# Transposes of an attention unit in one step, output transposes of global pairs joined with the next pair's, later loads of the globals, and a new order, in a fused attention and MLP kernel

## The chip, the cores and the metric

The kernel runs on one core of a Trainium2 chip. A core has five engines that run side by side, each through its own list of instructions in order: TensorE (PE in the profile) multiplies and transposes, VectorE (DVE), ScalarE (ACT) and GpSimd (POOL) work on elements, SyncE (SP) issues most of the DMAs here. The metric is the device time of one execution in microseconds (us). Before the change it is 1034.27 us, the median of three runs (1033.44 to 1035.80).

## What is computed

Attention over 8 batches, 8 heads, 512 local and 32 global positions, head size 64. A local query sees the 32 global keys and the local keys within 32 positions; a global query sees all 544 keys. Each batch's outputs, heads side by side, are 544 tokens of 512 numbers, 4352 tokens in all. They go through an MLP with a hidden size of 2048.

```python
s_g = scale * np.matmul(q_g, k_all.transpose(0, 1, 3, 2))
out_g = np.matmul(sm(s_g), v_all)
s_ll = np.where(mask, scale * np.matmul(q_l, k_l.transpose(0, 1, 3, 2)), -1000000000.0)
s_l = np.concatenate([scale * np.matmul(q_l, k_g.transpose(0, 1, 3, 2)), s_ll], axis=-1)
out_l = np.matmul(sm(s_l), np.concatenate([v_g, v_l], axis=2))
x = attn_out.transpose(0, 2, 1, 3).reshape(B * S, H * D)
h = x @ w_in
g = 0.5 * h * (1.0 + erf(h * inv_sqrt2))
return g @ w_out
```

## The kernel before

**Work.** The attention is cut into 64 *units* `(b, half, p)`: batch, half of the 512 local queries (256), pair of heads. The MLP runs in 17 *passes* over 256 tokens each: sixteen keyed `(b, half)`, and a last one, `"g"`, with the global tokens of all batches. Where numbers must stay exact to float32, a value is split into a high and a low part in a faster format (`fp32r`) and three products are summed; the first 12 units work in plain float32 instead.

**Steps.** All work is written as named steps, each with its function, engine, due time, what it needs, which buffers it takes and frees. The names that matter here:

- `lk`, `lq`, `lv`: loads of a unit's keys, queries and values (`lv` of unit (0,0,0) and of (0,1,0) load those of four units, into `vre`); `lg`: a batch's global queries and keys; `glv`: values for a global pair. All but one are issued by SP.
- `tk`, `tq`: transposes of keys and queries; `k1`, `q1`: copies of them; `s`: scores; `m`: mask and row minimum (DVE); `e`: exponential (ACT); `n`, `nf`, `ns`: normalisation (DVE, POOL).
- `t`: transposes of the normalised attention, `st_t` (L712). Seven matmuls of 128x128: four with j = 0, three with j = 1, each half into one slot of the PSUM pool `t`, which has two. `ah`, `al`: copies of them as high and low part (`ao` tiles in the first 12 units, `at` later); `o`: attention times values, whose results take slots of the same pool; `c`, `x`: sums of the results (tile `xs`).
- For a global pair `g = (b, x)` of four heads, with i = 0, 1 for its two head pairs: `gt`: five transposes of its attention (`gu_t`); `go`: times values; `gsh`, `gsl`: the result's parts summed into `os`; `gx`: its transpose (`gu_x`), one matmul; `gyh`, `gyl`, `gw`: parts summed (tile `gc`) and written to a DRAM buffer, from which the last pass starts.
- `wl`: load of one of 32 weight tiles of 0.5 MB (`wpair`, even numbers w_in, odd ones w_out); `w1`, `w2` (ACT), `w3` (DVE), `w4` (DVE or ACT), `w5` (DVE or POOL): the split of a pair of them. Pair n is made of weights n and n + 1 (n even) and belongs to hidden block f = n / 2. Five raw buffers serve the sixteen pairs.
- `h` (or `hc`, in quarters): up-projection of one hidden block, twelve matmuls (L963 to L965), tile `h`; `g`, `gh`, `gl`: its Gelu and the two parts; `mo`: down-projection, six matmuls (L995 to L997), tile `acc`.

**Order.** A planner walks through the steps when the program is built. It keeps a clock for each engine from the table of durations `DUR` and a model of the DMA from the loads' `size`, and of the steps that can start first it takes the one that is due first. Due times come from formulas, plus offsets by kind of step (`OFF`, `OFF0`) and by single step (`XO`). The result is one fixed order, and each engine runs its list strictly in it. So a step that waits holds up everything behind it on its engine.

**Start.** For the first 110 us the first eight units, the weights and the first pass run together. All of `w_in` and `w_out` stays on the chip afterwards.

Of the kernel before, what the change touches and what calls it, by code (L numbers as in the profile page):

```python
# [109 lines left out]
    ('gn', (0, 0)): -484.33, ('gn', (0, 1)): 234.3, ('go', (0, 0), 0): -396.25, ('go', (0, 0), 1): -58.92,  # L110
    ('go', (0, 1), 0): 174.43, ('go', (0, 1), 1): 24.38, ('gsh', (0, 0), 0): 229.87, ('gsh', (0, 0), 1): -56.02,
    ('gsh', (0, 1), 0): 290.46, ('gsh', (0, 1), 1): -341.29, ('gsl', (0, 0), 0): -143.39, ('gsl', (0, 0), 1): -123.39,
    ('gsl', (0, 1), 0): -70.91, ('gsl', (0, 1), 1): -75.86, ('gt', (0, 0)): -197.62, ('gt', (0, 1)): -44.95,
    ('gvc', (0, 0), 0): 575.55, ('gvc', (0, 0), 1): 539.98, ('gvc', (0, 1), 0): -62.66, ('gvc', (0, 1), 1): 295.35,
# [1339 lines left out]
```

## Time and profile before

| | |
|---|---|
| median of three runs | 1034.27 us |
| profiled execution | 1035.02 us |
| its span, first to last instruction | 1033.2 us |
| moved by DMA | 71.17 MB |
| mean granted clock of PE | 0.99 |

The page's slices (40 of 25.8 us each; a digit is the busy share in tenths) show a start that differs from the rest:

```profile
PE   7789999999999999999999999999999999999998
ACT  6789738888899989798899989888999979873231
PEclk9789999999999999999999999999999999999999
GB/s 195 245 165 292 55 38 64 65 61 75 48 36 66 58 73 39 68 56 71 46 37 65 60 71 39 70 55 72 43 40 59 65 71 47 33 24 43 1 22 21
```

In the first four slices the weights are loaded, PE is not yet full, and its granted clock is below full speed at times. From the fifth on PE is full and the DMA moves little. How long a group of instructions takes is read from the table by lines (count, busy time, mean duration of one, and the idle time ahead of it with what ended it), and what happened at a place from the timeline (start, duration, engine, line, operation, what it writes and reads).

### The profile page before, as it was taken

Reading aid. Unit: us, or ns where it says so; the run is one execution under the profiler, and the core shown is the slowest. Engines: PE = TensorE matmul, PEld = TensorE weight load, DVE = VectorE, ACT = ScalarE, POOL = GpSimd, SP = SyncE. Lnnn points to the kernel's source line nnn. Section 1 sums busy time; section 2 is a strip of 40 time slices with the busy share of each in tenths; the row PEclk is TensorE's granted clock in tenths of the full one; section 3 lists DMA queues with packets and bytes.
Section 4 is the critical chain, followed back from the end, with each engine's and each line's share of the span. In section 5 each row is a group of like instructions: output and inputs, shape, how many; then the busy total and the mean of one; then the engine's idle time right before and its main releaser. Section 6 shows DMA issues by size and latency. Waiting matters only on the chain.

```text
span 1033.2 us, 21240 instructions
## 1 busy us (share of the span) xinstructions
PE 1011.6 (98%) x6908; PEld 909.9 (88%) x6908; DVE 734.2 (71%) x2169; ACT 814.9 (79%) x1761; POOL 352.8 (34%) x399
## 2 busy tenths in 40 slices
PE   7789999999999999999999999999999999999998
PEld 4478888999999999999999999999999999999897
DVE  5688628896888988766888988866888888751000
ACT  6789738888899989798899989888999979873231
POOL 3332433343323433343323443343323443332221
PEclk9789999999999999999999999999999999999999
DMA  8869213333223232323222332323222332111000
GB/s 195 245 165 292 55 38 64 65 61 75 48 36 66 58 73 39 68 56 71 46 37 65 60 71 39 70 55 72 43 40 59 65 71 47 33 24 43 1 22 21
DMA packets 273135, 71.17 MB, mean 69 GB/s; under 512 B 258304, under 2 KB 266496, under 8 KB 273024
## 3 DMA queue, kind: packets, MB, share of 16 engines
q1 hardware_dynamic: 271872, 69.42, 29.3%
q8 instruction: 55, 0.90, 0.4%
q14 instruction: 56, 0.46, 0.2%
q10 hardware_dynamic: 1152, 0.39, 0.1%
HBM read 60.29 MB, written 9.44 MB: 67 GB/s over the span
## 4 chain that ended last, share of the span: by engine, by line
PE 93%; SPq 2%; DMA 2%; DVE 1%; ACT 1%; issue 0%; POOL 0%; ACTq 0%; DVEq 0%
PE h L963 12%; PE h L965 12%; PE h L964 12%; PE acc L995 12%; PE acc L996 12%; PE acc L997 12%; PE s L646 5%; PE o L753 5%; PE t L717 3%; PE go L886 2%; DMA wpair<-in_moe_w_out_dram 2%; PE sg L797 1%; PE t L718 1%; PE o L766 1%; PE gt L847 1%; PE t L720 1%
## 5 line engine op out<-in xcount | busy, mean ns | idle before, releaser
L311 POOL TENSOR_TENSOR gl<-gf,gh 128x512 fp32r<-128x512 f32 x135 | 179.3, 1328 | 421.7 <-ACT gh L301 306.0
L963 PE MATMUL h<-xx,w 128*128 128x256 f32 x1088 | 311.9, 287 | 1.8 <-DVE w L303 1.8
L965 PE MATMUL h<-xx,w 128*128 128x256 f32 x1088 | 304.2, 280 | 0.8 <-DVE w L311 0.8
L964 PE MATMUL h<-xx,w 128*128 128x256 f32 x1088 | 303.7, 279 | 0.0
L995 PE MATMUL acc<-w,gh 128*128 128x512 f32 x544 | 219.6, 404 | 0.0
L963 PEld LDWEIGHTS h<-xx,w 128*128 128x128 f32 x1088 | 204.8, 188 | 12.7 <-issue 3.3
L997 PE MATMUL acc<-w,gh 128*128 128x512 f32 x544 | 214.7, 395 | 0.0
L996 PE MATMUL acc<-w,gl 128*128 128x512 f32 x544 | 214.6, 395 | 0.0
L964 PEld LDWEIGHTS h<-xx,w 128*128 128x128 f32 x1088 | 205.0, 188 | 6.8
L965 PEld LDWEIGHTS h<-xx,w 128*128 128x128 f32 x1088 | 204.5, 188 | 1.0 <-DVE w L311 1.0
L481 ACT ACT_TABLE_LOAD x139 | 178.3, 1283 | 6.5 <-PE h L965 4.2
L481 ACT ACTIVATE gf<-h 128x512 f32<-128x512 f32 x136 | 81.4, 598 | 68.5 <-PE h L965 56.6
L997 PEld LDWEIGHTS acc<-w,gh 128*128 128x128 f32 x544 | 102.1, 188 | 24.5
L996 PEld LDWEIGHTS acc<-w,gl 128*128 128x128 f32 x544 | 102.5, 189 | 12.8 <-POOL gl L311 0.3
L995 PEld LDWEIGHTS acc<-w,gh 128*128 128x128 f32 x544 | 102.2, 188 | 12.9 <-issue 0.3
L481 ACT ACTIVATE a_t<-a_t,sm 128x192 f32<-128x192 f32 x240 | 109.9, 460 | 1.1 <-DVE sm L665 0.2
L311 POOL TENSOR_TENSOR vs<-vr,vs 128x512 fp32r<-128x512 f32 x52 | 68.5, 1317 | 105.1 <-DVE vs L303 47.1
L301 ACT ACTIVATE gh<-gf 128x512 fp32r<-128x512 f32 x110 | 69.4, 631 | 24.3 <-PE acc L997 21.6
L665 DVE CUSTOM_DVE_ANT_0 a_t<-s,mask 128x192 f32<-128x192 f32 x240 | 76.2, 368 | 16.7 <-PE s L646 15.9
L737 DVE TENSOR_TENSOR at<-t,at 128x512 fp32r<-128x512 f32 (+1 forms) x104 | 62.5, 615 | 28.3 <-ACT at L301 27.9
L301 ACT ACTIVATE at<-t 128x512 fp32r<-128x512 f32 (+1 forms) x104 | 54.1, 540 | 32.2 <-PE t L718 15.7
L311 POOL TENSOR_TENSOR vgs<-raws,vgs 128x640 fp32r<-128x640 f32 x32 | 51.1, 1597 | 77.3 <-ACT vgs L301 68.5
(148 smaller groups left out, 1730.2 us busy)
## 6 DMA issues: line engine op xcount, KB each, us to landing
wpair<-in_moe_w_in_dram SPq DMA_DIRECT2D x16, 512.0 KB, 5.9
wpair<-in_moe_w_out_dram SPq DMA_DIRECT2D x16, 512.0 KB, 6.3
...
raws<-in_k_l_dram SPq DMA_DIRECT2D x224, 36.0 KB, 2.0
raws<-in_q_l_dram SPq DMA_DIRECT2D x224, 32.0 KB, 1.9
...
```

The lines of the kernel that those rows point to most:

```text
L301: nc.scalar.activation(out=out, in_=in_, func=AF.Copy)
L311: (nc.vector if e == "v" else nc.gpsimd).tensor_sub(**kw)
L481: nc.scalar.activation(func=func, **kw)
L646: nc.tensor.matmul(out=st[u, "s", jj][:, c:c + w], lhsT=l, rhs=r, start=(i == 0 and n == 0), stop=(i == 1 and (plain or n == 1)), skip_gro ...
L665: nc.vector.tensor_tensor_reduce(out=a_t[:, j, aoff[half][i]:aoff[half][i] + w], in0=s[:, c:c + w], in1=masks[half][:, c:c + w], scale=-SC ...
L737: nc.vector.tensor_sub(out=at[:, 1], in0=st.pop((u, "t", j))[:, :n * P].rearrange("p (n q) -> p n q", q=P), in1=at.bitcast(F32)[:, 0])
L963: nc.tensor.matmul(out=h, lhsT=hi, rhs=xh, start=(c == 0), stop=False, skip_group_check=True)
L964: nc.tensor.matmul(out=h, lhsT=hi, rhs=xl, start=False, stop=False, skip_group_check=True)
L965: nc.tensor.matmul(out=h, lhsT=lo, rhs=xh, start=False, stop=(c == NCC - 1), skip_group_check=True)
L995: nc.tensor.matmul(out=acc[t], lhsT=gh[:, f % 2, tsl], rhs=hi, start=(f == a), stop=False)
L996: nc.tensor.matmul(out=acc[t], lhsT=gl[:, f % 2, tsl], rhs=hi, start=False, stop=False)
L997: nc.tensor.matmul(out=acc[t], lhsT=gh[:, f % 2, tsl], rhs=lo, start=False, stop=(f == b - 1))
```

## The change

Three edits of the code, new numbers for the planner, and the order that follows from them.

1. From the 13th unit on, the two `t` steps become one, `st_tt`, which issues the same seven transposes and takes both slots of the pool `t` at once. Both `ah` steps then need the one step.
2. The second output (i = 1) of a global pair is no longer transposed in a step of its own. The next pair's `gt` does it, into a free part of its own PSUM tile, so `gt` has six transposes in place of five (but for the first one) and needs `gsl` of the pair before. The transposes of i = 0, and the last pair's, stay. The due times of `gyh`, `gyl` and `gw` of the moved ones are 25 or 85 us later.
3. The planner's durations for the steps with transposes and for the plain float32 steps are longer, and its sizes of loads larger; the globals' load counts 0.6 where it counted 0.06.
4. All values of `OFF` and `XO` are new; `OFF0` and the planner's other constants stay.

```diff
-    "n": 1.15, "nf": {"p": 1.03, "v": 0.41}, "ns": {"p": 0.42, "v": 0.3}, "t0": 0.44, "t1": 0.33,
+    "n": 1.15, "nf": {"p": 1.03, "v": 0.41}, "ns": {"p": 0.42, "v": 0.3}, "t0": 0.52, "t1": 0.41, "t2": 0.85,
...
-    "m": -106.5, "mask": 329.5, "mo": 2.6, "n": -110.2, "nf": -113.8, "ns": -336.4, "o": -149.1,
+    "m": -145.2, "mask": 398.1, "mo": 3.2, "n": -116.4, "nf": -102.8, "ns": -303.2, "o": -119.6,
...
-    ('ah', (0, 0, 0), 0): -161.52, ('ah', (0, 0, 0), 1): 571.94, ('ah', (0, 0, 1), 0): 1841.53,
+    ('ah', (0, 0, 0), 0): -427.89, ('ah', (0, 0, 0), 1): 627.85, ('ah', (0, 0, 1), 0): 537.09,
...
+    def st_tt(e, u):
+        for j in range(2):
+            st_t(e, u, j)
...
+    def before(g):
+        b, x = g
+        return (b, 0) if x else (b - 1, 1) if b else None
...
         nc.tensor.transpose(out=tg[:, 0:P], in_=s[:, 128:128 + P], identity=ident)
+        pg = before(g)
+        if pg:
+            nc.tensor.transpose(out=tg[:, P:2 * P], in_=st[pg, 1, "os"].rearrange("p j e -> p (j e)"), identity=ident)
+            st[pg, 1, "x"] = tg[:, P:2 * P].rearrange("p (j l q) -> p j l q", j=2, l=2)
...
-            step(("lg", b), load_g, (b,), "s", s0 - 12.0, takes=[("kgr", b), ("qgr", b)], issues=8, size=0.06)
+            step(("lg", b), load_g, (b,), "s", s0 - 12.0, takes=[("kgr", b), ("qgr", b)], issues=8, size=0.6)
...
-        step(("t", u, 0), st_t, (u, 0), "t", f0 - 4.5, [("ns", u)] + pv(("o", 1)), [("t", (u, 0))], [("ge", u), (an, u)], dur="t0")
-        step(("t", u, 1), st_t, (u, 1), "t", f0 - 4.4, [("t", u, 0)], [("t", (u, 1))], [("ge", u), (an, u)], dur="t1")
+        if w:
+            step(("t", u, 0), st_t, (u, 0), "t", f0 - 4.5, [("ns", u)] + pv(("o", 1)), [("t", (u, 0))], [("ge", u), (an, u)], dur="t0")
+            step(("t", u, 1), st_t, (u, 1), "t", f0 - 4.4, [("t", u, 0)], [("t", (u, 1))], [("ge", u), (an, u)], dur="t1")
+        else:
+            step(("t", u), st_tt, (u,), "t", f0 - 4.5, [("ns", u)] + pv(("o", 1)), [("t", (u, 0)), ("t", (u, 1))], [("ge", u), (an, u)], dur="t2")
...
+                step(("ah", u, j), st_ah, (u, j), "a", f0 - 4.0 + 0.1 * j, [("t", u)], [("at%d" % j, u)], dur="ah%d" % j)
...
-            step(("gt", g), gu_t, (g,), "t", g0 + 2.0, [("gn", g), ("late",), ("go", pg, 1) if pg else None],
-                 [("s", (g, "t")), ("t", (g, "tg"))], [("sgr%d" % (p // 2), b)])
+            step(("gt", g), gu_t, (g,), "t", g0 + 2.0, [("gn", g), ("late",), ("go", pg, 1) if pg else None, ("gsl", pg, 1) if pg else None],
+                 [("s", (g, "t")), ("t", (g, "tg"))], [("sgr%d" % (p // 2), b)] + ([("gos", (pg, 1))] if pg else []), dur="gt" if pg else "gt0")
...
+                ng = ((b, 1) if not g[1] else (b + 1, 0) if b + 1 < B else None) if i else None
+                gd = g0 if ng is None else g0 - 5.0 + (30.0 if not g[1] else 90.0)
+                if ng is None:
+                    step(("gx", g, i), gu_x, (g, i), "t", g0 + 6.5 + 2 * i, [("gsl", g, i)], [("s", (g, i, "x"))], [("gos", (g, i))])
+                step(("gyh", g, i), gu_yh, (g, i), "a", gd + 7.0 + 2 * i, [("gx", g, i) if ng is None else ("gt", ng)], [("gc", (g, i))])
+                step(("gyl", g, i), gu_yl, (g, i), "v", gd + 7.3 + 2 * i, [("gyh", g, i)], [], [("s", (g, i, "x")) if ng is None else ("t", (ng, "tg"))])
```

What the order makes of it is shown at three places of the start. Line numbers of the changed kernel are lower by one in the functions up to `st_t` and higher by 11 behind `gu_t`.

The first is SP's list behind the second half's queries of batch 0 (`vr<-in_q_l`): `vre` are the first values, `kgr` and `qgr` batch 1's globals, `wpair` weights. Before:

```order
L520 DMA vr<-in_q_l_dram 128x8x64 x2
L437 DMA kgr<-in_k_g_dram 32x4x32 x4
L439 DMA qgr<-in_q_g_dram 32x8x32 x4
L453 DMA vre<-in_v_l_dram 128x8x64 x2
L461 DMA vre<-in_v_l_dram 32x8x64
L461 DMA vre<-in_v_g_dram 32x8x64
L461 DMA vre<-in_v_l_dram 64x8x64
L464 DMA vre<-in_v_g_dram 32x4x64 x2
L464 DMA vre<-in_v_l_dram 32x4x64 x2
L331 DMA wpair<-in_moe_w_in_dram 128x4x256
L335 DMA wpair<-in_moe_w_out_dram 128x1024
```

Now (the first row is weight 4, the last two are weights 5 and batch 1's globals' first half):

```order
L330 DMA wpair<-in_moe_w_in_dram 128x4x256
L519 DMA vr<-in_q_l_dram 128x8x64 x2
L452 DMA vre<-in_v_l_dram 128x8x64 x2
L460 DMA vre<-in_v_l_dram 32x8x64
L460 DMA vre<-in_v_g_dram 32x8x64
L460 DMA vre<-in_v_l_dram 64x8x64
L463 DMA vre<-in_v_g_dram 32x4x64 x2
L463 DMA vre<-in_v_l_dram 32x4x64 x2
L881 DMA raws<-in_v_l_dram 128x4x64 x2
L882 DMA raws<-in_v_g_dram 32x2x64
L334 DMA wpair<-in_moe_w_out_dram 128x1024
L436 DMA kgr<-in_k_g_dram 32x4x32 x4
```

Weight 4 moved ahead of the values, and batch 1's globals from ahead of the values to behind them.

The second is SP's list around weights 12 to 14, behind the value loads of unit 8. Before (`vr` are unit 9's values, `raws<-in_k_l` unit 8's keys; the second row of weights is 13, the third 14):

```order
L331 DMA wpair<-in_moe_w_in_dram 128x4x256
L453 DMA vr<-in_v_l_dram 128x2x64 x2
L461 DMA vr<-in_v_l_dram 32x2x64
L461 DMA vr<-in_v_g_dram 32x2x64
L461 DMA vr<-in_v_l_dram 64x2x64
L464 DMA vr<-in_v_g_dram 32x64 x2
L464 DMA vr<-in_v_l_dram 32x64 x2
L335 DMA wpair<-in_moe_w_out_dram 128x1024
L420 DMA raws<-in_k_l_dram 32x9x32 x4
L331 DMA wpair<-in_moe_w_in_dram 128x4x256
```

Now (`raws<-in_q_l` are unit 9's queries, the second row of keys are unit 9's):

```order
L419 DMA raws<-in_k_l_dram 32x9x32 x4
L424 DMA raws<-in_q_l_dram 32x8x32 x4
L330 DMA wpair<-in_moe_w_in_dram 128x4x256
L334 DMA wpair<-in_moe_w_out_dram 128x1024
L330 DMA wpair<-in_moe_w_in_dram 128x4x256
L419 DMA raws<-in_k_l_dram 32x9x32 x4
L452 DMA vr<-in_v_l_dram 128x2x64 x2
```

Unit 8's keys and unit 9's queries moved ahead of weight 12, and unit 9's values from between weights 12 and 13 to behind weight 14, with unit 9's keys; weight 15 comes behind those values.

The third is DVE's list from unit 0's mask step (`a_t,sm<-s,mask`) to its normalisation. Before:

```order
L665 ISA a_t_122,sm<-s,mask_92 128x224
L665 ISA sm 128x1
L303 COPY kq_138<-kp 128x320
L303 COPY sgr_129<-sg 64x288
L692 TENSOR_SCALAR sm<-sm 128x4
L693 RECIPROCAL sm<-sm 128x4
L696 TENSOR_TENSOR a_t_122<-a_t_122,sm 128x2x2x128
```

Now:

```order
L664 ISA a_t_122,sm<-s,mask_92 128x224
L664 ISA sm 128x1
L349 SCALAR_TENSOR_TENSOR wpair<-wpair 128x1024
L302 CAST w_249<-wpair 128x2x512
L310 TENSOR_TENSOR w_249<-wpair,w_249 128x2x512
L691 TENSOR_SCALAR sm<-sm 128x4
L692 RECIPROCAL sm<-sm 128x4
L695 TENSOR_TENSOR a_t_122<-a_t_122,sm 128x2x2x128
```

The two copies left this place, and the three DVE steps of weight pair 0 (`w3`, and `w4` and `w5`, which ACT and POOL did) stand there instead.

More of the change, by code (lines that the diff above doesn't have):

```diff
@@ L27 @@
     "tgh": 0.62, "tgl": 0.77, "s": 0.87, "m": 0.7, "sg": 0.27, "sgc": 0.4, "sgz": {"a": 0.42, "v": 0.42}, "sga": 0.43, "e": 0.92,
[1 row of a table removed]
[1 row of a table added]
     "ah0": 0.6, "al0": 0.69, "ah1": 0.5, "al1": 0.56, "vm": 0.3, "vc": {"v": 0.43, "a": 0.63}, "vl": {"p": 1.32, "v": 0.65},
[1 row of a table removed]
-    "gmin": 0.92, "gex": 0.8, "gn": 0.88, "gt": 0.57, "gah": 0.38, "gal": 0.42, "gagh": 0.25, "gagl": 0.27,
[1 row of a table removed]
[1 row of a table added]
+    "gmin": 0.92, "gex": 0.8, "gn": 0.88, "gt": 0.74, "gt0": 0.64, "gah": 0.38, "gal": 0.42, "gagh": 0.25, "gagl": 0.27,
[1 row of a table added]
     "xh": {"v": 0.3, "a": 0.4}, "xl": {"v": 0.42, "p": 0.72}, "h": 1.42, "hc": 0.355, "g": 0.62, "gh": {"a": 0.63, "v": 0.44},
@@ L50 @@
 OFF = {
-    "ah": -111.4, "al": 46.7, "c": -38.8, "e": 162.2, "g": -22.3, "gagh": -31.6, "gagl": 50.2,
-    "gah": -40.0, "gal": 445.8, "gex": -32.1, "gh": -11.3, "gl": 124.7, "glv": -384.9, "gmin": 465.3,
[7 rows of a table removed]
+    "ah": -35.4, "al": 39.5, "c": -23.6, "e": 186.2, "g": -5.6, "gagh": -79.4, "gagl": 85.5,
+    "gah": -137.1, "gal": 331.2, "gex": -172.8, "gh": -96.3, "gl": 151.8, "glv": -466.8, "gmin": 572.1,
[5 rows of a table added]
+    "sga": 144.0, "sgc": 105.8, "t": -315.2, "tc1": 124.9, "tg": -300.5, "tgh": 347.3, "tgl": -409.1,
+    "tk": 57.2, "tq": 177.3, "vc": 28.9, "vl": 183.4, "vm": 346.4, "x": -96.9, "xh": -27.5, "xl": -462.6,
 }
@@ L110 @@
[L110 to L114, printed above, removed]
@@ L115 @@
-    ('gvc', (1, 0), 0): 91.69, ('gvl', (0, 0), 0): 53.83, ('gvl', (0, 0), 1): 115.55, ('gvl', (0, 1), 0): -318.54,
[3 rows of a table removed]
-    ('gyh', (0, 1), 0): 107.58, ('gyh', (0, 1), 1): 477.1, ('gyl', (0, 0), 0): -647.88, ('gyl', (0, 0), 1): 106.83,
[56 rows of a table removed]
-    ('sga', (0, 0, 1)): -384.3, ('sga', (0, 0, 2)): 532.83, ('sga', (0, 0, 3)): 336.28, ('sga', (0, 1, 0)): -530.75,
-    ('sga', (0, 1, 1)): -716.14, ('sga', (0, 1, 2)): -379.73, ('sga', (0, 1, 3)): 58.21, ('sga', (1, 0, 0)): -68.75,
-    ('sga', (1, 0, 1)): -410.36, ('sga', (1, 0, 2)): -381.48, ('sga', (1, 0, 3)): 44.57, ('t', (0, 0, 0), 0): -237.68,
[6 rows of a table removed]
@@ L185 @@
-    ('tg', 0): -609.81, ('tg', 1): -420.0, ('tgh', 1): -1094.83, ('tgl', 0): 564.55, ('tgl', 1): 300.08,
[37 rows of a table removed]
[18 rows of a table added]
+    ('gagh', (0, 1)): -215.12, ('gagl', (0, 0)): -763.25, ('gagl', (0, 1)): -15.95, ('gah', (0, 0), 0): 142.37,
+    ('gah', (0, 0), 1): 201.56, ('gah', (0, 1), 0): -169.41, ('gah', (0, 1), 1): 201.63, ('gal', (0, 0), 0): -615.26,
+    ('gal', (0, 0), 1): -1182.59, ('gal', (0, 1), 0): 583.14, ('gal', (0, 1), 1): -805.68, ('gex', (0, 0)): 294.16,
[7 rows of a table added]
+    ('glv', (0, 0), 1): 924.69, ('glv', (0, 1), 0): 777.82, ('glv', (0, 1), 1): 870.73, ('glv', (1, 0), 0): 631.8,
@@ new lines @@
+    ('glv', (1, 0), 1): 611.15, ('gmin', (0, 0)): -1351.29, ('gmin', (0, 1)): 892.35, ('gn', (0, 0)): 241.11,
+    ('gn', (0, 1)): -142.5, ('go', (0, 0), 0): -51.34, ('go', (0, 0), 1): 229.73, ('go', (0, 1), 0): 256.54,
+    ('go', (0, 1), 1): 284.76, ('gsh', (0, 0), 0): 155.13, ('gsh', (0, 0), 1): 403.53, ('gsh', (0, 1), 0): 50.17,
+    ('gsh', (0, 1), 1): 42.22, ('gsl', (0, 0), 0): 323.37, ('gsl', (0, 0), 1): 29.18, ('gsl', (0, 1), 0): 203.52,
+    ('gsl', (0, 1), 1): -253.19, ('gt', (0, 0)): 479.16, ('gt', (0, 1)): 208.91, ('gvc', (0, 0), 0): 68.13,
@@ new lines @@
+    ('gvc', (0, 0), 1): 198.46, ('gvc', (0, 1), 0): -270.95, ('gvc', (0, 1), 1): 72.5, ('gvc', (1, 0), 0): -172.22,
+    ('gvl', (0, 0), 0): 14.44, ('gvl', (0, 0), 1): 754.46, ('gvl', (0, 1), 0): 502.95, ('gvl', (0, 1), 1): 304.66,
+    ('gvl', (1, 0), 0): 549.86, ('gw', (0, 0), 0): 460.52, ('gw', (0, 0), 1): 608.56, ('gw', (0, 1), 0): 493.49,
+    ('gw', (0, 1), 1): 493.51, ('gx', (0, 0), 0): -186.43, ('gx', (0, 1), 0): 236.64, ('gyh', (0, 0), 0): 209.45,
+    ('gyh', (0, 0), 1): 182.4, ('gyh', (0, 1), 0): 159.28, ('gyh', (0, 1), 1): 477.1, ('gyl', (0, 0), 0): -265.23,
@@ L223 @@
+    ('gyl', (0, 0), 1): -609.09, ('gyl', (0, 1), 0): -199.49, ('gyl', (0, 1), 1): -359.33, ('h', (0, 0), 1): 501.11,
[56 rows of a table added]
+    ('sga', (0, 0, 2)): 547.23, ('sga', (0, 0, 3)): 234.02, ('sga', (0, 1, 0)): 329.79, ('sga', (0, 1, 1)): -62.15,
+    ('sga', (0, 1, 2)): -1093.31, ('sga', (0, 1, 3)): -212.04, ('sga', (1, 0, 0)): -500.03, ('sga', (1, 0, 1)): 130.43,
[45 rows of a table added]
 }
@@ L1115, in attn_mlp @@
                 z = units[n - 1 - units[n - 1][2] % (2 if units[n - 1][1] in QUAD else 4)] if n else None
-                step(("lk", u), load_kn, (u, m), LKE[n], s0 - 15.0, [], [], issues=2 + half + 1 + m // 2, size=0.25 * m, after=("lk", z) if n else None)
-                step(("lq", u), load_qn, (u, m), LQE[n], s0 - 14.0, [], [], issues=2, size=0.22 * m, after=("lq", z) if n else None)
+                step(("lk", u), load_kn, (u, m), LKE[n], s0 - 15.0, [], [], issues=2 + half + 1 + m // 2, size=0.4 * m, after=("lk", z) if n else None)
+                step(("lq", u), load_qn, (u, m), LQE[n], s0 - 14.0, [], [], issues=2, size=0.25 * m, after=("lq", z) if n else None)
             step(("tk", u), st_tkn, (u,), "t", s0 - 5.0, [("lk", ld)] + pv(("tq",)), [("h", (u, "k"))], dur="tkn")
@@ L1163, in attn_mlp @@
             else:
-                step(("ah", u, j), st_ah, (u, j), "a", f0 - 4.0 + 0.1 * j, [("t", u, j)], [("at%d" % j, u)], dur="ah%d" % j)
+                step(("ah", u, j), st_ah, (u, j), "a", f0 - 4.0 + 0.1 * j, [("t", u)], [("at%d" % j, u)], dur="ah%d" % j)
                 step(("al", u, j), st_al, (u, j), "v", f0 - 3.5 + 0.1 * j, [("ah", u, j)], [], [("t", (u, j))], dur="al%d" % j)
         if n < NPE and p == 0:
-            step(("lv", u), load_v, (u, NP), LVE[half], f0 - 18.0, [], [], issues=9, size=1.8, after=("lv", units[0]) if n else None)
+            step(("lv", u), load_v, (u, NP), LVE[half], f0 - 18.0, [], [], issues=9, size=2.3, after=("lv", units[0]) if n else None)
             step(("vm", u), st_vm, (u, NP), "p", f0 - 8.0, [("lv", u)], dur="vm8")
         elif n >= NPE:
-            step(("lv", u), load_v, (u,), "s", f0 - 18.0, [("o", units[n - 2], 1)] if n >= NPE + 2 else [("tq", units[NPE - 1])], [("vr%d" % odd, u)], issues=9, size=0.46, after=("lv", z if n > NPE else units[4]))
+            step(("lv", u), load_v, (u,), "s", f0 - 18.0, [("o", units[n - 2], 1)] if n >= NPE + 2 else [("tq", units[NPE - 1])], [("vr%d" % odd, u)], issues=9, size=0.55, after=("lv", z if n > NPE else units[4]))
             step(("vm", u), st_vm, (u,), "p", f0 - 8.0, [("lv", u)])
@@ L1204, in attn_mlp @@
                 step(("gsl", g, i), gu_sl, (g, i), "v", g0 + 5.8 + 2 * i, [("gsh", g, i)], [], [("s", (g, i, "o"))])
-                step(("gx", g, i), gu_x, (g, i), "t", g0 + 6.5 + 2 * i, [("gsl", g, i)], [("s", (g, i, "x"))], [("gos", (g, i))])
-                step(("gyh", g, i), gu_yh, (g, i), "a", g0 + 7.0 + 2 * i, [("gx", g, i)], [("gc", (g, i))])
-                step(("gyl", g, i), gu_yl, (g, i), "v", g0 + 7.3 + 2 * i, [("gyh", g, i)], [], [("s", (g, i, "x"))])
-                step(("gw", g, i), gu_w, (g, i), "s", g0 + 8.0 + 2 * i, [("gyl", g, i)], [], [("gc", (g, i))], issues=1, size=0.02)
+                ng = ((b, 1) if not g[1] else (b + 1, 0) if b + 1 < B else None) if i else None
[4 more added lines that the diff above has]
+                step(("gyl", g, i), gu_yl, (g, i), "v", gd + 7.3 + 2 * i, [("gyh", g, i)], [], [("s", (g, i, "x")) if ng is None else ("t", (ng, "tg"))])
+                step(("gw", g, i), gu_w, (g, i), "s", gd + 8.0 + 2 * i, [("gyl", g, i)], [], [("gc", (g, i))], issues=1, size=0.02)
     LAG = LAGS
```

5 lines of the change are left out of this document (removed), and 266 rows, old and new, of tables (DUR, OFF, XO).

## The prediction

> **What bounds the kernel now.** The first view is the head of the profile's page: the span, then each engine's busy time.
>
> ```profile
> span 1033.2 us, 21240 instructions
> PE 1011.6 (98%) x6908; PEld 909.9 (88%) x6908; DVE 734.2 (71%) x2169; ACT 814.9 (79%) x1761; POOL 352.8 (34%) x399
> ```
>
> The profiled execution took 1035.02 us: the span of 1033.2 and 1.8 around it. The median of the runs, 1034.27, is 0.75 lower. PE is busy for 98% of the span, but an average hides where the other 21.6 us lie. The table by stretches shows it (length of the stretch, then busy time of PE, PEld, DVE, ACT and POOL, then the granted clock of PE, DMA share and GB/s):
>
> ```profile
> 0.00:76.30 76.30, 59.41 (x355) 40.10 (x356) 53.13 (x158) 56.94 (x132) 27.73 (x56) 0.87 0.75 200
> 31.90:38.70 6.80, 6.31 (x32) 4.49 (x34) 1.94 (x4) 2.34 (x3) 0.97 (x2) 0.50 0.94 319
> 72.90:76.30 3.40, 3.40 (x23) 2.84 (x23) 1.02 (x5) 3.38 (x11) 2.76 (x2) 0.50 0.92 301
> 76.30:106.60 30.30, 30.30 (x214) 26.43 (x213) 26.14 (x31) 29.82 (x34) 8.22 (x8) 1.00 0.83 262
> 106.60:1029.00 922.40, 921.86 (x6343) 843.37 (x6341) 654.88 (x1983) 727.62 (x1596) 316.81 (x336) 1.00 0.24 51
> ```
>
> From 106.6 to 1029.0 PE idles for 0.5 us of 922.4. So only the start can give time: 16.9 us of idle PE before 76.3 (76.30 - 59.41), and the stretches at half clock, two of which are shown (0.50); the mean of 0.87 makes them a quarter of the first 76.3 us, about 20 us. From 76.3 to 106.6 PE is full, but ACT is full beside it (29.82 of 30.30): there ACT splits the weights that PE uses next, and both set the pace. Two waits of PE, from the list that puts the longest first, name what the start waits for:
>
> ```profile
> PE kp L528 <- DMA kn<-in_k_l_dram: 5.0, 2, 3.7
> PE h L963 <- DVE w L303: 1.8, 1, 1.8
> ```
>
> The first is the arrival of the first keys, which both kernels load first. The other is an up-projection that waited for its weights.
>
> **The change, part by part.** *Seven transposes in one step.* No instruction is added or removed. What a run of transposes costs, and what changing from one kind of matmul to another costs, is read from starts:
>
> ```profile
> 510.26 0.27 PE L718 MATMUL t<-ident,ge 128*128 128x128 f32 x1
> 510.37 0.27 PE L720 MATMUL t<-ident,ge 128*128 128x128 f32 x1
> 510.40 0.48 PE L995 MATMUL acc<-w,gh 128*128 128x512 f32 x1
> 510.72 0.40 PE L996 MATMUL acc<-w,gl 128*128 128x512 f32 x1
> 510.96 0.39 PE L997 MATMUL acc<-w,gh 128*128 128x512 f32 x1
> ```
>
> One transpose follows another at 0.11 us. From the last one's start to the second acc matmul's start it is 0.35 us, which is one transpose (0.11) and one acc matmul (0.24, as between the last two rows). So the change of kind costs nothing to within 0.01 us, and joining 52 pairs of steps gives 0, with bounds of 0.5 us to either side. The price could be a wait: the step now takes both slots of the PSUM pool `t` at once. In the new order at least one down-projection step and some up-projection matmuls, 3.5 us of PE work, stand between the previous unit's last `o` and these transposes, and 2.8 us between the transposes and their own `o` (0.6 before). I take 0; if that cover went, every one of the 52 units would wait.
>
> *Global outputs.* 15 `gx` transposes move into the next pair's `gt` step; 0.11 us each, the same number: 0. They no longer stand right behind a wait for ACT and DVE. The table loads fall from 140 to 122 in the new order, none of the 18 before the weights are done:
>
> ```profile
> L481 ACT ACT_TABLE_LOAD x139 | 178.3, 1283 | 6.5 <-PE h L965 4.2
> ```
>
> That is 18 x 1.283 = 23 us of ACT time after 106.6, where ACT is busy 727.62 of 922.40 and PE waits for nothing: 0.
>
> *The new order at the start, SP.* Here is all that can count. Rows of SP's issues, start and duration:
>
> ```profile
> 18.17 4.29 SPq L437 DMA_DIRECT2D kgr<-in_k_g_dram  x4
> 22.50 1.91 SPq L439 DMA_DIRECT2D qgr<-in_q_g_dram  x4
> ...
> 30.36 0.90 SPq L464 DMA_DIRECT2D vre<-in_v_l_dram  x2
> 31.31 0.43 SPq L331 DMA_DIRECT2D wpair<-in_moe_w_in_dram  x1
> ...
> 36.28 3.60 SPq L425 DMA_DIRECT2D raws<-in_q_l_dram  x4
> 40.94 4.41 SPq L453 DMA_DIRECT2D vre<-in_v_l_dram  x2
> ...
> 55.76 1.02 SPq L453 DMA_DIRECT2D vr<-in_v_l_dram  x2
> ...
> 60.50 0.42 SPq L335 DMA_DIRECT2D wpair<-in_moe_w_out_dram  x1
> 60.97 1.92 SPq L420 DMA_DIRECT2D raws<-in_k_l_dram  x4
> ...
> 65.69 1.80 SPq L425 DMA_DIRECT2D raws<-in_q_l_dram  x4
> ```
>
> The eight issues of batch 1's globals hold SP for 6.2 us (18.17 to 24.41), and the first values (to 31.26) and weight 4 (31.31) are issued behind them. Now weight 4 goes ahead of the values and both ahead of the globals. So the values are out by 31.3 - 6.2 = 25.0 at the latest, and weight 4, which is freed of the values' 6.9 us too, by 18.2. What that frees:
>
> ```profile
> 32.39 1.15 PE L766 MATMUL o<-ao,vre 128*64 128x128 f32 x4 [0.76 <-DMA vre<-in_v_l_dram]
> 49.44 0.48 PE L717 MATMUL t<-ident,ae 128*128 128x128 f32 x1 [2.38 <-ACT ao L301]
> 36.75 1.14 ACT L342 ACTIVATE wpair<-wpair 128x1024 int32<-128x1024 uint16 x1 [2.79 <-DMA wpair<-in_moe_w_out_dram]
> ```
>
> Against it stands a block on DVE: the three steps of weight pair 0 now all run there, ahead of unit 0's normalisation. By the rows below they take 1.23 + 0.69 + 1.23 = 3.2 us. So units 0 to 4 run up to 3 us later, and the first `o` ends not 6 but about 1.2 us earlier (the 0.76 of DMA wait, and some of the half-clock work behind it). From there on the DMA waits are what is missing: ACT's 2.79 at 36.75 goes, and of PE's 2.38 at 49.44, whose copy stands on ACT behind that work, between 0 and all; I take 1.4, nearer to all. PE's side of the start thus gains 1.2 + 2.8 + 1.4 = **5.4 us** by the transposes of unit 3.
>
> *What is late next: the weights.* Weight 13 is issued at 60.50, behind unit 9's nine value loads that begin at 55.76 (4.7 us). Now unit 8's keys (1.92) and unit 9's queries (1.80) stand there: 1.0 us less. SP's two long holds before (3.60 at 36.28, and 4.41 for two issues at 40.94) came with eight weights of 0.5 MB just issued; now six are. 1 MB at the 319 GB/s of 31.9 to 38.7 is 3.1 us, and I take 2.5. So weight 13 comes 3.5 us earlier, and with it ACT's first step on pair 12. Behind it on ACT:
>
> ```profile
> 66.01 1.13 ACT L342 ACTIVATE wpair<-wpair 128x1024 int32<-128x1024 uint16 x1
> 69.74 1.15 ACT L342 ACTIVATE wpair<-wpair 128x1024 int32<-128x1024 uint16 x1 [1.58 <-DMA wpair<-in_moe_w_out_dram]
> 105.59 1.23 DVE L350 SCALAR_TENSOR_TENSOR wpair<-wpair 128x1024 int32<-128x1024 int32 x1 [0.38 <-ACT wpair L346]
> 107.99 0.69 DVE L303 CAST w<-wpair 128x1024 fp32r<-128x1024 f32 x1
> 108.72 1.23 DVE L311 TENSOR_TENSOR w<-wpair,w 128x1024 fp32r<-128x1024 f32 x1
> 110.36 0.28 PE L963 MATMUL h<-xx,w 128*128 128x256 f32 x1
> ```
>
> The order puts unit 8's exponentials and pair 12's cast ahead of pair 14, so the idle 1.58 at 69.74 is filled: 1.6 more. Two copies of globals (0.5) move in behind pair 12: -0.5. One cast more for DVE instead of ACT (pair 14) and two `ao` copies more for ACT: 0 on ACT, 0.7 on DVE at most, of which I count 0.5. The rest of the list to 106.6 is the same work on a full engine, so the gain is carried to the end: 3.5 + 1.6 - 0.5 - 0.5 = 4.1. The last weights were ready at 109.95 and PE took them at 110.36, so there is almost no cushion: PE can gain no more than the weights and no more than its own side, the smaller of 5.4 and 4.1. I say **4.0 us**. From that point all is as before, the tail too (its steps stand in the same order). Against the profiled execution this is 1031.0, against the median, 0.75 lower, **1030.3**.
>
> *Bounds of this term.* Least: the queue drains as before (2.5 gone) and the idle time moves to weight 15, which is issued about 1 us later now (1.6 gone): 0. Most: 5.4 and a half-clock stretch (3.40 us of busy PE, so 1.7) less: 7.1.
>
> **Rivals.** *Swallowed.* The lower bound: SP's order helps only its 1.0 us and ACT, full either way, hands on nothing more. Time 1034.3 - 1.0 = 1033.3. For it: ACT's 29.82 of 30.30. Against it: ACT's waits for weights (2.79, 1.58) are real and stand before that.
>
> *Slower: the DVE block decides.* If values and weights come early but unit 0 to 4 are what PE's order waits for, the 3.2 us on DVE are paid in full by every later step, and SP's tighter order of unit 8's loads (four key loads wait for DVE's transposes of the unit before) holds the weights back as well. Then PE is 3.2 later, less the 0.76 of DMA wait: +2.4, 1036.7. It decides where the first `o` starts after 33.0. For it: PE's waits for DVE and ACT copies in the first 30 us. Against it: 2.79 us of ACT idle behind a late DMA.
>
> *The merged step waits in the steady part.* If both slots come free 0.3 us late at each of 52 units: +15.6, 1049.9. Against it: the 3.5 us of cover.
>
> *The clock.* A longer run of transposes could end the full clock: one 3.4 us stretch at half clock (as at 72.9) after each of 52 runs would cost 1.7 us each, 88 us: 1122. Against it: the granted clock is 1.00 from 106.6 to 1029.0 with runs of four. [...] No run here shows a run of seven yet.
>
> **How the numbers follow.** The forecast has 0.60 (its own range 1027.2, the upper bound of the gain, to 1032.2), swallowed 0.22, slower by DVE 0.14, the merged step's wait 0.03, the clock 0.01. 0.2% is 2.07 us, about what a measurement of this kernel tells from no change. Faster than 1032.2 is the forecast, 0.60; within 0.2% the swallowed case, 0.22; slower the rest, 0.18. The range reaches from 1027.2 to 1035.5, which takes in the swallowed case with 2 us for its size, and leaves the slower ones out.
>
> **What would show it.** Right: the first values' DMAs issued near 17 to 24; no DMA wait in the first `o`; ACT's step on pair 4 with no wait; weight 13 issued near 57.5; the last pair's final DVE step ending near 106 and PE's last first-pass up-projection right behind it; PE full after it, with no wait at `t`. Wrong: SP's holds near 36 to 45 as long as before, ACT idle ahead of pair 14, the first `o` after 33, waits of `t` on DVE `xs`, or a clock below 1.00 after 110.

## The result: 0.9% slower

The change takes 1044.80 us (median of 4 runs, 1042.93 to 1045.99) against 1035.03 us before (4 runs, 1033.44 to 1036.91): a ratio of 1.0092 with a 95% interval of 1.0067 to 1.0117. The forecast was 1030.3, the range 1027.2 to 1035.5. The profiled execution took 1045.66 us, its span is 1043.8 (before 1035.02 and 1033.2).

The head of the profile after, and its slices of PE, of PE's granted clock and of the DMA:

```profile
span 1043.8 us, 21207 instructions
PE 1016.5 (97%) x6908; PEld 912.2 (87%) x6908; DVE 750.1 (72%) x2184; ACT 780.1 (75%) x1711; POOL 364.2 (35%) x416
...
PE   6899999999999999999999999999999999999998
...
PEclk9699999999999999999999999999999999999999
...
GB/s 226 209 176 277 47 54 66 68 45 63 58 45 79 35 77 41 72 40 52 64 46 78 37 75 46 67 47 51 64 43 77 41 75 45 35 23 43 1 21 21
```

In tenths nothing seems to differ behind the start. The table by stretches (its columns as before) is finer:

```profile
0.00:76.30 76.30, 61.89 (x363) 41.80 (x364) 53.78 (x162) 56.60 (x132) 25.25 (x53) 0.84 0.77 201
76.30:106.60 30.30, 29.15 (x207) 24.97 (x206) 25.43 (x26) 29.84 (x36) 8.29 (x9) 1.00 0.80 259
106.60:116.00 9.40, 9.40 (x65) 8.57 (x65) 7.40 (x10) 5.07 (x12) 3.82 (x3) 1.00 0.14 31
116.00:1029.00 913.00, 905.85 (x6230) 828.58 (x6229) 662.82 (x1988) 686.19 (x1529) 325.62 (x351) 1.00 0.25 52
```

PE, which idled for 0.5 us from 106.6 to 1029.0 before, now idles for 913.00 - 905.85 = 7.2 us. The list of waits of PE after 110 us has four lines, with the total, the number and the longest; before, it had a single wait of 0.3:

```profile
PE t L716 <- DVE gc L925: 3.0, 5, 0.6
PE s L645 <- DVE kq L310: 1.9, 2, 1.2
PE sg L800 <- DVE sm L664: 1.9, 5, 0.7
PE s L645 <- DVE sgr L818: 0.4, 1, 0.4
```

Five waits of the joined transposes `t`, five of the global scores `sg`, and three of `s`. The engine is DVE each time.

**The lag of PE.** Idle time in a profile begins where the model puts the end of a matmul, so it understates a wait (at the place below 0.59 us are shown, where the rows give 0.81). For all that follows I use a number that is made of the rows: the distances between the ends of successive PE instructions, less the usual distance for that shape in the profile before (0.117 us for an up-projection matmul, 0.233 for a down-projection, 0.109 for a transpose), summed from the start. It is how far PE is behind a run without any wait at the usual distances, so slow matmuls at a lower clock in the start count in it too (at a granted clock of 0.50 one transpose follows another at 0.22 us in the profile before, 34.86 to 35.08). The last matmul ends at 1003.0 us plus the lag.

| kernel | ratio to before (95%) | lag at 110 us | at the end | gained after 110 us |
|---|---|---|---|---|
| before | 1 | 24.5 | 25.9 | 1.4 |
| the change | 1.0092 (1.0067 to 1.0117) | 24.4 | 36.2 | **11.8** |
| e11, the change again | 1.0092 (1.0075 to 1.0108) | 23.0 | 34.6 | 11.7 |
| e1, its code, old numbers | 1.0062 (1.0041 to 1.0083) | 27.5 | 37.4 | 9.8 |
| e2, old code, its numbers | 1.0120 (1.0101 to 1.0138) | 22.9 | 39.0 | 16.1 |
| e3, five `t` covered | 1.0024 (1.0012 to 1.0035) | 22.5 | 28.6 | 6.0 |
| e4, all covered | 0.9987 (0.9975 to 0.9999) | 22.0 | 24.7 | 2.7 |
| e5, weight block behind | 1.0014 (1.0002 to 1.0026) | 23.8 | 26.3 | 2.5 |
| e6, globals first | 1.0002 (0.9993 to 1.0012) | 22.8 | 25.3 | 2.5 |
| e7, old order, joined | 1.0157 (1.0143 to 1.0172) | 25.2 | 42.8 | 17.6 |
| e8, ACT relieved | 1.0070 (1.0055 to 1.0085) | 27.3 | 31.9 | 4.6 |
| e9, four more covers | 0.9995 (0.9984 to 1.0006) | 21.2 | 24.3 | 3.0 |
| e10, split at five places | 1.0095 (1.0077 to 1.0113) | 24.2 | 37.3 | 13.1 |

By these rows the whole loss lies after 110 us: 11.8 - 1.4 = 10.4 us, against 10.6 between the two profiled executions. The start, on which the prediction rests, is level in this pair of profiles (24.4 and 24.5).

**What the waits are.** One of the five places of `t`, first PE's rows and then DVE's (start, duration, line, operation):

```profile
363.94 0.33 PE L719 MATMUL t<-ident,ge 128*128 128x128 f32 x1
364.86 0.41 PE L716 MATMUL t<-ident,a_t 128*128 128x128 f32 x2 [0.59 <-DVE gc L925]
```

```profile
363.60 0.29 DVE L707 TENSOR_TENSOR ge<-a_t,sm 128x128 f32<-128x128 f32 x1
363.81 0.42 DVE L302 CAST gh<-gf 128x512 fp32r<-128x512 f32 x1
364.14 0.27 DVE L875 TENSOR_TENSOR agg<-gtg,agg 32x128 fp32r<-32x128 f32 x1
364.34 0.38 DVE L925 TENSOR_TENSOR gc<-gtg,gc 64x32 f32<-64x32 f32 x2
364.75 0.42 DVE L866 TENSOR_TENSOR agt<-gt,agt 128x256 fp32r<-128x256 f32 x1
```

The four transposes have run; the three need the second slot of the pool `t`. It holds `gtg`, the second tile of `gt`, until DVE has read it twice: for `agg` (`gagl`), and for `gc` (`gyl`), which is the moved output of the pair before. DVE comes to that only behind the unit's normalisation and a cast. From 363.94 to 364.86 it is 0.92 us where one transpose follows another at 0.11: 0.81 lost, of which the idle column shows 0.59. The cover between `gt` and these transposes is two up-projections and a down-projection. By the planner's own clock it fits to a hair:

```
PE  357.35 gt(2,1)      PE  362.33 t(3,0,1)
DVE 361.51 gagl(2,1)    DVE 361.78 gyl(2,0),1, which ends at 362.17
```

0.16 us lie between the end of `gyl` and `t`, of which the planner counts 0.15 for the signal. On the chip DVE is later than planned, and its rows show by what:

```profile
358.86 1.28 POOL L310 TENSOR_TENSOR vs<-vr,vs 128x512 fp32r<-128x512 f32 x1 [3.29 <-PE h L976]
358.91 1.57 DVE L310 TENSOR_TENSOR kq<-kt,kq 64x320 fp32r<-64x320 f32 x1
```

This subtraction of the keys (`k2`) has a median of 0.49 us over its 104 instructions. Here it takes 1.57 beside POOL's subtraction of the values (`vl`), which started 0.05 us before it, and so it is at all five places (1.57 to 1.58). The planner never lets these two steps overlap: it puts `vl` behind `k2`. From there to `gc` DVE has no gap of more than 0.04 us, so without the 1.09 us above the median `gc` would have ended at 363.63, before PE came to the transposes that wait (364.05). That is worked out from the rows; no run moves the POOL step. The waits of `s` have such a step right ahead of them too (0.91 us at 173.08 and 0.98 at 233.12, for 0.49), those of `sg` have none in the 4 us before.

The cover is not shorter than it was, either. In the kernel before, 4.2 us of PE work stand between `gtg` and the same three transposes at three units, and nothing waits:

```profile
359.59 0.27 PE L848 MATMUL gtg<-ident,sgr 128*128 128x128 f32 x1
360.81 1.52 DVE L703 TENSOR_TENSOR ge<-a_t,sm 128x256 f32<-128x256 f32 x1
363.00 0.24 DVE L864 TENSOR_TENSOR agg<-gtg,agg 32x128 fp32r<-32x128 f32 x1
364.38 0.38 PE L717 MATMUL t<-ident,a_t 128*128 128x128 f32 x2
```

A step of DVE was stretched there too (1.52 us, where its median is 0.42), but DVE had read the tile 3.65 us after `gtg` started, 1.1 us ahead of PE. In the change the new order has more of DVE's work ahead of that reading: `agg` ends 5.34 us after `gtg` starts, and the moved `gc` 5.65, when PE has been waiting since about 5.0. So the margin is what went; how much of it the joined steps, the moved outputs and the new numbers each took is not shown, since no run has the moved outputs without the joined steps.

At the five `sg` the plan is as tight: `sg` stands one up-projection (1.4 us) behind its unit's `s`, and the mask step that frees its slot is planned to end 0.31 us ahead of it.

### The profile page after: what moved, and what is told of

Read it like the earlier page. It is cut to its first block, busy times and chain, and to the rows that moved or that the text cites. A ratio compares the mean times of both kernels' runs of the same rounds, so it can differ in the third digit from the quotient of the medians.

```text
span 1043.8 us, 21207 instructions
## 1 busy us (share of the span) xinstructions
PE 1016.5 (97%) x6908; PEld 912.2 (87%) x6908; DVE 750.1 (72%) x2184; ACT 780.1 (75%) x1711; POOL 364.2 (35%) x416
## 4 chain that ended last, share of the span: by engine, by line
PE 76%; DVE 8%; ACT 6%; issue 3%; DMA 3%; SPq 2%; POOL 1%; DVEq 0%; ACTq 0%; POOLq 0%
PE acc L1006 10%; PE acc L1007 10%; PE acc L1008 10%; PE h L974 10%; PE h L976 9%; PE h L975 9%; PE s L645 5%; PE o L756 4%; PE t L716 2%; PE go L897 2%; DMA vr<-in_v_l_dram 1%; PE sg L800 1%; PE t L717 1%; ACT L480 1%; DVE kq L310 1%
## 5 line engine op out<-in xcount | busy, mean ns | idle before, releaser
L974 PEld LDWEIGHTS h<-xx,w 128*128 128x128 f32 x1088 | 204.4, 188 | 10.6 <-issue 1.6
L300 ACT ACTIVATE gh<-gf 128x512 fp32r<-128x512 f32 x100 | 63.3, 633 | 41.0 <-PE acc L1008 39.3
L740 DVE TENSOR_TENSOR at<-t,at 128x512 fp32r<-128x512 f32 (+1 forms) x104 | 62.1, 618 | 25.9 <-ACT at L300 25.0
L645 PE MATMUL s<-kq 128*128 128x192 f32 (+1 forms) x480 | 68.7, 306 | 4.6 <-DVE sm L664 2.3
```

Of the source, the lines that this page charges most:

```text
L300: nc.scalar.activation(out=out, in_=in_, func=AF.Copy)
L645: nc.tensor.matmul(out=st[u, "s", jj][:, c:c + w], lhsT=l, rhs=r, start=(i == 0 and n == 0), stop=(i == 1 and (plain or n == 1)), skip_gro ...
L740: nc.vector.tensor_sub(out=at[:, 1], in0=st.pop((u, "t", j))[:, :n * P].rearrange("p (n q) -> p n q", q=P), in1=at.bitcast(F32)[:, 0])
L974: nc.tensor.matmul(out=h, lhsT=hi, rhs=xh, start=(c == 0), stop=False, skip_group_check=True)
```

## Experiments

### Does covering the waits give the loss back?

In e3 one up-projection is moved ahead of `t` at the five places; nothing else in the order differs. The list of steps is changed when the planner has made it:

```diff
     order.sort(key=lambda e: e[:2])
+    names = [e[2]["name"] for e in order]
+
+    def ahead(x, y):
+        i, j = names.index(x), names.index(y)
+        if i > j:
+            names.insert(j, names.pop(i))
+            order.insert(j, order.pop(i))
+
+    for b in range(2, 7):
+        ahead(("h", (b, 1), 4), ("t", (b + 1, 0, 1)))
```

> The change with one up-projection step (1.40 us of PE) moved ahead of the joined transposes at the five places where they wait for the slot that gt's second tile holds. Nothing else in the order differs. If the wait is for that slot and nothing else is late (theory A or B alike): the five waits of 0.59 us in the idle time (0.78 + 0.17 in the pitch of PE's instructions) go, 4.8 us less, 1040.0. Theory C (a wait that is covered comes back one step later, at the results of that unit): 1043 to 1045, with waits of o for al in the same five places.

e4 adds:

```diff
+    for b in range(2, 7):
+        ahead(("mo", (b, 0), 7), ("sg", (b + 1, 0, 0)))
+    for x in (("mo", (0, 1), 11), ("hc", (0, 1), 15, 2)):
+        ahead(x, ("s", (1, 1, 1)))
```

> As the run before, and besides one down-projection step (1.40 us) moved ahead of the global scores sg at five units, and 1.75 us of other work ahead of the scores of unit (1,1,1). If the waits after 110 us are the whole loss: 4.8 + 3.2 + 1.8 = 9.8 us less than the change, 1035.0, level with before, and PE's lag at 110 us the same as in before. Theory C: 1040 or more.

Measured: e3 1038.26 us beside 1036.34 of before, ratio 1.0024; e4 1035.02, ratio 0.9987. PE's waits after 110 us, first e3, then e4:

```profile
PE sg L800 <- DVE sm L664: 1.9, 5, 0.6
PE s L645 <- DVE kq L310: 1.7, 2, 1.1
...
```

```profile
PE o L756 <- DVE at L740: 0.5, 1, 0.5
PE s L645 <- DVE sgr L818: 0.4, 1, 0.4
PE s L645 <- DVE kq L310: 0.2, 1, 0.2
```

The five of `t` are gone in e3, and so are those of `sg` in e4. After 110 us the lag grows by 6.0 and 2.7 us instead of 11.8: 5.8 and 9.1 given back, of 4.8 and 9.8 expected. Nothing comes back one step later, but for 0.5 at one `o`. With twelve PE steps moved, the changed code is level with before (the interval of e4 ends at 0.9999). So neither the joined steps nor the other new places cost anything that more cover doesn't remove. e11, the change itself with runs of its own, shows the same loss a second time:

> The change itself once more, on the same chip as the two above: 0.8 to 1.0% slower than before, with PE's lag at 110 us between 22 and 24.5 us (24.4 in its first profile, 22.0 and 22.5 in the two covered orders, whose lists are the same up to there) and 11 to 12 us more of it at the end.

### Is it the joining that waits?

e10 takes the joined step apart at the five places alone: the four transposes stay, the three come 2 us of PE later.

```diff
+    for b in range(2, 7):
+        u = (b + 1, 0, 1)
+        i = names.index(("t", u))
+        x = order[i][2]
+        order[i] = (*order[i][:2], dict(x, fn=st_t, args=(u, 0)))
+        j = names.index(("mo", (b, 0), 14)) + 1
+        names.insert(j, ("t", u, 1))
+        order.insert(j, (*order[i][:2], dict(x, fn=st_t, args=(u, 1), takes=[("t", (u, 1))])))
```

> The change with the joined transposes taken apart at the five places where they wait for the slot of gt's second tile: the four stay, the three stand behind the next output of the global pair and the next down-projection (2.0 us of PE later). Nothing else differs. If the joining is what costs there (theory J): the five waits go, 4.8 us less than the change. If DVE is late there whatever the transposes need (theory O: the order leaves too little work between gt and what waits for DVE's copies of it): the next step, go, waits 1 us for its own copy from the same list of DVE in place of it, and the time is level with the change within 1.5 us.

Measured: ratio 1.0095, the same as the change (1.0092), with 13.1 us of lag gained. Its largest wait, and the same place in its timeline:

```profile
PE go L897 <- DVE agt L866: 5.2, 5, 1.1
...
364.89 0.71 PE L897 MATMUL go<-vgs,agt 128*128 128x256 f32 x4 [1.05 <-DVE agt L866]
```

The wait has only changed its owner. `go` needs `agt`, the next instruction in DVE's list, and waits 1.05 us in place of the transposes' 0.59. So at these places the joined step is where the wait shows, not its cause: DVE is late for everything that stands behind `gt`, and the order has too little PE work there for it. The stretched `k2` stands ahead of these five waits as well (1.57 to 1.60 us).

e7 puts the question to the old order: its list is kept, but the work between the four and the three transposes goes ahead of them in all 52 units.

```diff
+    pe = [x for x in names if x in nodes and nodes[x]["on"] == "t"]
+    for u in units[NF32:]:
+        i, j = pe.index(("t", u, 0)), pe.index(("t", u, 1))
+        for x in pe[i + 1:j]:
+            ahead(x, ("t", u, 0))
```

> The kernel before with its whole order kept, but in each of the 52 units from the 13th on what stood between the four and the three transposes is moved ahead of them, so that all seven stand together. If joining costs nothing by itself: within 1 us of before, ratio 0.999 to 1.001. If a joined step waits for its second slot as a rule: 0.3 us at each unit, 15 us longer; if it does so only behind gt: 0.6 to 0.8 us at up to 14 units, 5 to 10 us longer.

Measured: ratio 1.0157, 16 us slower, 17.6 us of lag after 110. Its longest lines:

```profile
PE o L753 <- DVE at L737: 5.2, 13, 0.6
PE t L717 <- DVE xs L779: 3.6, 3, 1.2
```

No expectation had this form; the 15 us of the second one are met in size only. The wait for the second slot is there at three units (3.6 us), but more is lost at the results `o`, at 13 units, which wait for the low parts `at` of the transposes: with the piece of work gone from between the transposes it no longer covers the copies. The transposes themselves cost what they did (0.11 us from one to the next in both kernels); what joining takes is a place for cover, and an order that was made for two steps hasn't got it elsewhere.

### The code or the numbers?

e1 is the change's code with before's durations, offsets and sizes, e2 the reverse. In short, of e1:

```diff
-    "n": 1.15, "nf": {"p": 1.03, "v": 0.41}, "ns": {"p": 0.42, "v": 0.3}, "t0": 0.52, "t1": 0.41, "t2": 0.85,
+    "n": 1.15, "nf": {"p": 1.03, "v": 0.41}, "ns": {"p": 0.42, "v": 0.3}, "t0": 0.44, "t1": 0.33, "t2": 0.77,
...
-    "m": -145.2, "mask": 398.1, "mo": 3.2, "n": -116.4, "nf": -102.8, "ns": -303.2, "o": -119.6,
+    "m": -106.5, "mask": 329.5, "mo": 2.6, "n": -110.2, "nf": -113.8, "ns": -336.4, "o": -149.1,
```

> The two joined steps of the change (transposes of a unit, output transpose with the next pair's attention) with all planner numbers of before. Theory A (the loss is in the order that the new numbers make, the joined steps cost nothing by themselves): within 3 us of before, 1032 to 1038, and few or no waits of t for a copy of the globals' output. Theory B (the joined step, which takes both slots of the pool t, waits by itself): waits of t behind gt once or more per batch, 5 us or more in all after 110 us, 1039 to 1046.

> The steps of before with all planner numbers of the change (durations, offsets, load sizes). Theory A: the waits after 110 us are there as in the change, about 10 us of them, 1041 to 1047. Theory B: the waits of t are gone and half or more of the loss with them, 1034 to 1040.

Measured: 1.0062 and 1.0120. Neither pairing is level with before, and no `t` waits for the globals' copies in e1. The line with the most idle time of e1, then of e2, after 110 us:

```profile
PE go L898 <- DVE agt L867: 1.2, 1, 1.2
```

```profile
PE t L716 <- DVE xs L778: 2.5, 4, 1.1
```

Theory B falls with e1: its time, 1042.99 us, lies in B's range, but B's waits of `t` behind `gt` are not there. Of theory A the part on e2 held in the main (16 us of lag where 10 were expected, and 1047.86 us, just above its range), the part on e1 did not: with the old numbers the joined steps are 6 us off, too. Each of these orders has its own scattered waits, 10 to 16 us of them after 110 us, and the order of before has nearly none. The numbers shift which steps meet; none of the two sets is right or wrong by itself.

### What sets the start?

On top of e4, e5 puts the three DVE steps of weight pair 0 behind unit 0's `ao` copies, and e6 the globals' loads ahead of the first values again (`behind_of` is the counterpart of `ahead`, `u0` the first unit).

```diff
+    for x, y in ((("w3", 0), ("ah", u0, 1)), (("w4", 0), ("w3", 0)), (("w5", 0), ("w4", 0))):
+        behind_of(x, y)
```

> The covered order of e4_cover_all, with the three DVE steps of weight pair 0 (3.2 us) put behind unit 0's ao copies instead of ahead of its normalisation. Theory D (that block holds unit 0 to 4 and sets the start): the first o starts 2 us earlier than in e4_cover_all and PE's lag at 110 us is 2 us smaller, time 1033. Theory E (the splits of the last weights, on a full ACT, set the end of the start whatever stands in its first 40 us): the first o earlier, the lag at 110 us the same within 1 us, time 1035.0 within 1.

```diff
+    ahead(("lg", 1), ("lv", units[0]))
```

> The covered order with the loads of batch 1's globals put back ahead of the first values on SP. If the later globals are what the start gains by (my prediction's step): the values are issued about 5 to 6 us later, the first o starts near 38 to 40, and the time is 2 to 4 us longer, 1037 to 1039. Theory E: the first o later, but the time within 1 us of e4_cover_all, 1034 to 1036.

Measured: 1.0014 and 1.0002, where e4 has 0.9987. e5 doesn't decide between D and E. Both expected the first `o` earlier; it starts at 34.80, 3.0 us later than in e4. In its new place the block stands ahead of the next units' masks on DVE, and PE waits for a copy behind them:

```profile
29.47 0.69 PE L527 MATMUL kp<-ident,kn 128*128 128x128 f32 x2 [4.03 <-DVE kq L302]
34.80 1.10 PE L769 MATMUL o<-ao,vre 128*64 128x128 f32 x16
```

So what D forecast, 2 us less, isn't met, but the block was never out of PE's way; and the time is 0.27% or 2.8 us above e4's, more than E's "within 1". In e6 the values are issued later by 4.8 us, yet the first `o` runs no later, which neither expectation had. Of each, the last issue of values and the first `o`, e4 and then e6:

```profile
24.67 0.91 SPq L463 DMA_DIRECT2D vre<-in_v_l_dram  x2
31.77 1.87 PE L769 MATMUL o<-ao,vre 128*64 128x128 f32 x16
```

```profile
29.50 1.02 SPq L463 DMA_DIRECT2D vre<-in_v_l_dram  x2
31.64 1.10 PE L769 MATMUL o<-ao,vre 128*64 128x128 f32 x16
```

The first `o` stands behind other PE work, not behind the values. What the later globals are worth in all, 0.15% or 1.5 us between e6 and e4, is within the two intervals, and theory E's "within 1 us" is not settled either.

e8 relieves ACT by `w4` of four weight pairs, and gives their `w5` to POOL.

```diff
+    for m in (18, 22, 26, 28):
+        nodes["w4", m]["on"], nodes["w5", m]["on"] = "v", "p"
```

> The covered order with w4 of the pairs 18, 22, 26 and 28 on DVE instead of ACT and their w5 on POOL instead of DVE: 4.4 us less for ACT and 2.2 us less for DVE before 110 us, 9.6 us more for POOL. Theory E (a full ACT sets the end of the start): the last weights are ready 2 to 4 us earlier, PE's lag at 110 us falls by 2 to 3 us, time 1032 to 1033. Theory D: no change within 1 us, since PE's own waits before 75 us stand.

Measured: 1.0070, slower, with the lag at 110 us at 27.3. The run doesn't answer the question, since it made another bound: PE waits for POOL's `w` (3.2 us at three places from 90 to 120), and DVE for POOL (2.55 us at 99.84, 2.29 at 109.07, 2.59 at 112.38). Where it starts:

```profile
86.67 3.37 POOL L310 TENSOR_TENSOR w<-wpair,w 128x1024 fp32r<-128x1024 f32 x1 [5.59 <-DVE w L302]
...
87.76 2.84 DVE L302 CAST w<-wpair 128x1024 fp32r<-128x1024 f32 x1
```

### Can it beat before?

> The covered order of e4_cover_all with four more steps of PE moved ahead: a quarter of an up-projection ahead of the scores of unit (1,1,1), the next quarter ahead of the results of unit (1,1,0), an up-projection ahead of the scores of unit (2,0,2), and one ahead of the results of unit (1,0,0). The waits there in e4_cover_all are 0.4, 0.8, 0.6 and 1.2 us; the last is followed by weights that leave 0.7 us. If covers are what is missing: 0.4 + 0.5 + 0.6 + 0.7 = 2.2 us less than e4_cover_all, which is 3.5 us or 0.34% less than before. If what is covered comes back elsewhere: level with e4_cover_all, 0.1% less than before.

```diff
+    ahead(("hc", (0, 1), 15, 3), ("s", (1, 1, 1)))
+    ahead(("hc", (1, 0), 0, 0), ("o", (1, 1, 0), 0))
+    ahead(("h", (1, 1), 4), ("s", (2, 0, 2)))
+    ahead(("h", (0, 0), 10), ("o", (1, 0, 0), 1))
```

Measured: 0.9995, and 3.0 us of lag gained after 110, not less than e4's 2.7. What was covered there comes back elsewhere: the wait at the `s` of unit (1,1,1) is gone, and new ones of 0.2 and 0.3 us of idle time stand at an `o` and a `go`. No version beats before clearly; e4 is 0.13% faster, hardly clear of no change.

## Why the prediction was wrong

**The step that failed** is "From that point all is as before", and under it "I take 0" for the joined transposes and for the outputs. The sum put 0 on everything after 110 us; it measured +10.4 us (11.8 against 1.4). Two things were wrong in it.

- The cover was counted to one tenant of the pool only. "3.5 us of PE work, stand between the previous unit's last `o` and these transposes": that holds in the new order but for unit (1,1,0), which has 1.75; but the pool's other tenant is `gt`'s second tile, which the change itself makes live longer, and which DVE in the new order reads 2.0 us later than before (5.65 against 3.65 us after `gtg`). The rival of the merged step's wait had the right mechanism with 0.03, as 0.3 us at all 52 units; it showed as 0.8 us at five. e10 shows that another step waits in its place when the step is split.
- A full PE was taken as a sign that any other order would keep it full. It was full because in that order the other engines were in time at nearly every point where PE depends on them. e1, e2 and e7 are three other orders, and each loses 10 to 18 us at such points. The five `sg` and the `s` of unit (1,1,1) are not in the prediction at all.

**The start** went the right way and was too large: -4.0 forecast. The change's list up to there ran in five profiles with a lag of 24.4, 23.0, 22.5, 22.0 and 24.2 us at 110 us (the change, e11, e3, e4, e10), a mean of 23.2; before's list in two, 24.5 and 25.2 (before, e7). That is 1.6 us less, with a scatter as large. By steps:

- *SP's order* came nearly as forecast: weight 4 is issued at 15.01 (forecast 18.2 at the latest), the last values to 26.15 (25.24 + 0.91; forecast 25.0 at the latest).

```profile
15.01 0.43 SPq L330 DMA_DIRECT2D wpair<-in_moe_w_in_dram  x1
...
25.24 0.91 SPq L463 DMA_DIRECT2D vre<-in_v_l_dram  x2
...
37.25 3.77 SPq L424 DMA_DIRECT2D raws<-in_q_l_dram  x4
41.82 4.25 SPq L452 DMA_DIRECT2D vre<-in_v_l_dram  x2
...
59.98 0.50 SPq L334 DMA_DIRECT2D wpair<-in_moe_w_out_dram  x1
```

- *The first `o` 1.2 us earlier* didn't come. It ended at 33.54 before (32.39 + 1.15); it ends at 35.63 in the change's profile (33.65 + 1.98), and at 33.64 in e4, whose list is the same so far (31.77 + 1.87). It no longer waits for a DMA, but other work stands in its place, and that work is slow: from 25 to 35 us the granted clock of PE is 0.50 in the change's profile, where it was 0.68.

```profile
33.65 1.98 PE L769 MATMUL o<-ao,vre 128*64 128x128 f32 x16
67.88 1.17 ACT L341 ACTIVATE wpair<-wpair 128x1024 int32<-128x1024 uint16 x1
75.61 1.15 ACT L341 ACTIVATE wpair<-wpair 128x1024 int32<-128x1024 uint16 x1
108.35 1.22 DVE L310 TENSOR_TENSOR w<-wpair,w 128x1024 fp32r<-128x1024 f32 x1
```

- *The 2.8 and the 1.4.* ACT's step on weights 4 and 5 has no wait any more, but starts at 35.25, 1.5 us earlier. PE's wait of 2.38 at 49.44 is gone, and one of 2.54 at 47.40, for a mask step of DVE, stands in its stead: the 1.4 came to nothing.
- *Weight 13* is issued at 59.98, 0.5 us earlier and not 3.5 (57.0; the prediction's list of signs has 57.5), since SP's two long holds stayed (3.77 at 37.25 and 4.25 at 41.82, before 3.60 and 4.41). ACT's steps on pairs 12 and 14 start at 67.88 and 75.61 (66.01 and 69.74 before): the new order fills ACT with other work ahead of them. That work isn't wasted, as the last weights are ready at 109.57 against 109.95. With ACT busy for 29.84 of 30.30 us from 76.3 to 106.6, this is the "swallowed" rival in this profile. In e4's the last weights come at 107.2.
- *No stall at `go`* behind 113 us any more: 0.5 us, not forecast.

**The tables of ACT** (121 loads) and **the transposes' own time** were right at 0. **The clock** rival is out: the rows give 1.00 from 116 to 1029 with runs of seven transposes, so none of these runs ended the full clock.
